# Two bookkeeping steps of an attention loop, placed later among its units

## The chip, the cores and the metric

The kernel runs on one core of a Trainium2 chip. The metric is the time of one execution on the device, in microseconds (us). A second number, the span, is what the profiler records from the first to the last instruction of one profiled execution; it is a little shorter than that execution's time.

## What is computed

Two blocks follow each other. The first is block-sparse attention over 4 batches, 8 heads, 768 tokens and 64 channels, with a mask made of 32 by 32 blocks. The second takes its output as 3072 rows of 512 numbers, gives each row to one of 8 experts by cosine similarity, and applies that expert's two-layer network.

```python
def _attn_ref(q, k, v, sampled_blocks):
    scores = np.matmul(q, k.transpose(0, 1, 3, 2)) / np.sqrt(D)
    ...
    scores = np.where(mask, scores, -1000000000.0)
    ...
    attn = np.exp(scores)
    attn = attn / (np.sum(attn, axis=-1, keepdims=True) + 1e-09)
    return np.matmul(attn, v)

def _moe_ref(x, expert_emb, tau, w1, w2):
    xn = x / (np.linalg.norm(x, axis=-1, keepdims=True) + 1e-06)
    en = expert_emb / (np.linalg.norm(expert_emb, axis=-1, keepdims=True) + 1e-06)
    logits = xn @ en.T / tau
    expert_idx = np.argmax(logits, axis=1)
    ...
    for e in range(E):
        mask = expert_idx == e
        h = np.maximum(x[mask] @ w1[e], 0.0)
        out[mask] = gate_w[mask, None] * (h @ w2[e])
```

## The kernel before

The attention handles heads in pairs: 16 pairs, four to a batch. Each pair has two halves of 384 queries, and each half runs over six chunks of 128 keys. One chunk of one half is a unit, so a half is 6 units, a pair 12, a batch 48, and there are 192 units. The loop in `attention_fast` (line 605) goes over them and issues, for each unit, the work of that unit and pieces of work that belong to other units.

The steps, with the names that the profile uses:

- `score_fast` (line 280) computes a unit's scores on TensorE into the tile `sc` (line 290), first the mask as a product of small bf16 matrices, then the queries and keys. ACT then takes the exponential into `e` (line 293). It is issued two units ahead. The pool of `sc` has two buffers, that of `e` four.
- `attend_fast` (line 297) adds `e` into a running sum `esum` on DVE (line 306 for the second unit of a half, line 308 for the later four) and multiplies `e` by the values into the accumulator `av` on TensorE (line 311). There is one accumulator buffer. At the sixth unit ACT copies one part of it (`part`, line 315) and DVE adds the two parts into `at` (line 317). The first `av` of the next half overwrites the accumulator, so it comes after that.
- `turn_fast` (line 260) turns half of the next pair's keys and queries by small matmuls into the tile `turn` (line 273). DVE copies the keys out (`kt`, line 276), ACT the queries (`qt`, line 277). It stands at the end of a half's sixth unit.
- `settle` (line 321) finishes a half. TensorE turns `at` back into rows of tokens and sums `esum` into denominators, both in the tile `back` (lines 339 and 346). DVE makes the denominators and their reciprocals (`dens` and `inv`, lines 349 to 352), the scaled rows `x` (line 354) and the products with the expert vectors (`part`, line 361, a second tile of that name). POOL squares `x` (`sq`, line 359), and DVE sums the squares (`nsq`, line 360).
- `route` (line 400) follows when a batch is complete. It is a chain of small operations on DVE with a power on POOL (`nrm`, line 410), which picks an expert for each token (`oh`, line 431). On ACT it takes one exponential of its logits `l` (line 434). The routed rows then go to memory by a DMA on the SP queue (line 438).
- `rank` (line 444) counts how many earlier tokens chose the same expert: six additions on POOL (`seen`, line 451), two products on TensorE into the tile `rk` (lines 453 and 454), and two DVE operations that read it (`mine` and `rank`, lines 455 and 456).

The tiles `turn`, `back` and `rk` all come from one pool, `small`, which has a single buffer of two banks; each of them waits until the one before has been read:

```python
def two_banks(k, name):
    return k.small.tile([P, 2, 512], F32, name=name, tag="small")
```

The order of the instructions on each engine's queue is made by a planner, which goes by the order of the program and by when it reckons an instruction to be ready. A queue then runs in that order. DVE's queue, for instance, has the sum of a half's second unit ahead of the copy `kt`, though the program issues `kt` first.

After the loop the last half is settled and the last batch routed and ranked (lines 620 to 622). `dispatch` then sorts the tokens into tiles of 128 by expert, and `experts` runs 27 of them (tiles `hp`, `h`, `yp`, `y`), with weights streamed from memory.

Of the kernel before, what the change touches and what calls it, by code (L numbers as in the profile page):

```python
# [23 lines left out]
NC = S // P  # L24
NPAIR = H // 2
# [31 lines left out]
def build_consts(k):  # L57
    nc, pool = k.nc, k.const
    k.ident = pool.tile([P, P], F32, name="ident")
    make_identity(nc, k.ident[:])  # L60
    k.ones = pool.tile([P, P], F32, name="ones")
    nc.vector.memset(k.ones, 1.0)
    k.half = pool.tile([P, NC], F32, name="half")
    nc.vector.memset(k.half, 0.5)

    k.before = pool.tile([P, P], F32, name="before")
    nc.gpsimd.memset(k.before, 1.0)
    nc.gpsimd.affine_select(out=k.before, in_=k.before, pattern=[[1, P]], compare_op=ALU.is_ge,
                            fill=0.0, base=-1, channel_multiplier=-1)
    k.rev = iota(k, "rev", [P, E], [[-1, E]], base=E)  # L70
    k.lane = iota(k, "lane", [P, P], [[1, P]])
    k.by_g = iota(k, "by_g", [P, N // G], [[G, N // G]])
    k.by_p = iota(k, "by_p", [P, NS + 1], [[P, NS + 1]])
    k.tile_no = iota(k, "tile_no", [P, NG], [[1, NG]])
    k.tok = iota(k, "tok", [P, NT], [[S, B], [1, NC]], base=-N, mult=NC)

    k.oh = pool.tile([P, NT, E], F32, name="oh")
    k.rank = pool.tile([P, NT], F32, name="rank")
    k.seen = pool.tile([P, NT + 1, E], F32, name="seen")
    nc.vector.memset(k.seen[:, 0, :], 0.0)  # L80


def load_ids(k):
    nc, pool = k.nc, k.setup
    k.ids = pool.tile([NB, NRAND], I32, name="ids")
    words = dataclasses.replace(k.blocks.tensor, shape=[NB, 2 * NRAND], dtype=I32)
    with nc.allow_non_contiguous_dma(reason="low words of the block numbers"):
        nc.sync.dma_start(out=k.ids, in_=bass.AP(tensor=words, offset=0, ap=[[2 * NRAND, NB], [2, NRAND]]))
# [57 lines left out]
def load_experts(k):  # L146
    nc, pool = k.nc, k.setup
    k.emb_rows = pool.tile([E, DM], F32, name="emb")
    nc.sync.dma_start(k.emb_rows, k.emb[:, :])
    k.tau_rows = pool.tile([E, 1], F32, name="tau")  # L150
    nc.sync.dma_start(k.tau_rows, bass.AP(tensor=k.tau.tensor, offset=0, ap=[[0, E], [1, 1]]))


def build_experts(k):
    nc, pool = k.nc, k.setup
    emb, tau = k.emb_rows, k.tau_rows
    sq = pool.tile([E, DM], F32, name="emb_sq")
    nrm = pool.tile([E, 1], F32, name="emb_nrm")
    nc.scalar.activation(sq, emb, ACT.Square, accum_out=nrm)
    nc.gpsimd.tensor_tensor(out=nrm, in0=nrm, in1=k.half[0:E, 0:1], op=ALU.pow)  # L160
    nc.vector.tensor_scalar(out=nrm, in0=nrm, scalar1=1e-6, scalar2=tau[:, 0:1], op0=ALU.add, op1=ALU.mult)
    nc.vector.reciprocal(out=nrm, in_=nrm)
    nc.vector.tensor_scalar(out=emb, in0=emb, scalar1=nrm[:, 0:1], scalar2=None, op0=ALU.mult)
    tp = two_banks(k, "tp")[:, 0]
    for c in range(ND):
        nc.tensor.transpose(tp[:, c * E:(c + 1) * E], emb[:, c * P:(c + 1) * P], k.ident[0:E, 0:E])
    k.en = k.const.tile([P, ND, E], F32, name="en")
    nc.vector.tensor_copy(out=k.en, in_=tp[:, 0:ND * E].rearrange("p (c e) -> p c e", e=E))
    k.back = k.const.tile([P, NPAIR, D + E], F32, name="back")
    for h in range(2):  # L170
        rows = slice(D * h, D * (h + 1))
        nc.vector.tensor_copy(out=k.back[rows, :, 0:D],
                              in_=k.ident[rows, rows].unsqueeze(1).broadcast_to([D, NPAIR, D]))
        nc.vector.tensor_copy(out=k.back[rows, :, D:D + E], in_=k.en[rows])


def load_pair(k, g, parts=(0, 1, 2), engine=None):
    b, j = g // NPAIR, g % NPAIR
    got = k.loaded.setdefault(g, [None, None, None])
    for i in parts:  # L180
        name, src = (("k", k.k), ("q", k.q), ("v", k.v))[i]
        t = k.ld.tile([P, 2, NC, D], F32, name=f"{name}ld", tag=f"{name}ld")
        (engine or k.nc.sync).dma_start(
            out=t.rearrange("p h c d -> p h (c d)"),
            in_=src[b, 2 * j:2 * j + 2].rearrange("h (p c) d -> p h (c d)", c=NC),
        )
        got[i] = t
# [72 lines left out]
def turn_fast(k, g, part):  # L260

    nc = k.nc
    if part == 0:
        k.turned[g] = [k.tp.tile([P, NC, 2, D], F32, name=f"{n}t", tag=f"{n}t") for n in ("k", "q")]
    ps = two_banks(k, "turn")[:, :, 0:2 * NQ * D].rearrange("p r (n c t) -> p r n c t", n=2, t=D)
    chunks = slice(part * NQ, (part + 1) * NQ)
    for n in range(2):
        src = k.loaded[g][n]
        for c in range(NQ):
            for r in range(2):  # L270
                toks = slice(D * r, D * (r + 1))
                for h in range(2):
                    nc.tensor.matmul(ps[D * h:D * (h + 1), r, n, c, :], lhsT=src[toks, h, part * NQ + c, :],
                                     rhs=k.ident[toks, toks], start=True, stop=True)
    kt, qt = [t[:, chunks].rearrange("p c r t -> p r c t") for t in k.turned[g]]
    nc.vector.tensor_copy(out=kt, in_=ps[:, :, 0])  # L276
    nc.scalar.mul(out=qt, in_=ps[:, :, 1], mul=SCALE)  # L277


def score_fast(k, u):  # L280

    nc = k.nc
    g, qh, kc = u // (2 * NC), u // NC % 2, u % NC
    kt, qt = [t.rearrange("p c r t -> p (c r t)") for t in k.turned[g]]
    ps = k.big.tile([P, 2, 512], F32, name="sc", tag="big")
    queries = slice(qh * HALF, (qh + 1) * HALF)
    quarters = [(h, r, slice(kc * P + D * r, kc * P + D * (r + 1))) for r in range(2) for h in range(2)]
    for rows, cols, first in ((k.kmask, k.qmask, True), (kt, qt, False)):
        for h, r, keys in quarters:
            nc.tensor.matmul(ps[D * r:D * (r + 1), h, 0:HALF], lhsT=rows[D * h:D * (h + 1), keys],  # L290
                             rhs=cols[D * h:D * (h + 1), queries], start=first, stop=not first)
    e = k.ep.tile([P, 2, HALF], F32, name="e", tag="e")
    nc.scalar.activation(e, ps[:, :, 0:HALF], ACT.Exp)  # L293
    k.es[u] = e
# [284 lines left out]
def attention_fast(n, ctx):  # L579
    def pool(name, bufs, **kw):  # L580
        return ctx.enter_context(n.tc.tile_pool(name=name, bufs=bufs, **kw))

    n.big, n.acc = pool("big_f", 2, space=PSUM), pool("acc", 1, space=PSUM)
    n.ld, n.tp, n.ep, n.sp = pool("ld", 3), pool("tp", 2), pool("ep", 4), pool("sp", 3)
    n.xp, n.rp = pool("xp", 2), pool("rp", 2)
    pairs = B * NPAIR
    units, per = pairs * 2 * NC, 2 * NC
    with n.tc.tile_pool(name="setup", bufs=1) as n.setup:
        load_ids(n)
        load_pair(n, 0, (0,))  # L590
        load_pair(n, 0, (1,), n.nc.scalar)
        load_pair(n, 0, (2,))
        load_experts(n)
        load_pair(n, 1)
        build_consts(n)
        build_mask(n)
        build_experts(n)
    zero = n.const.tile([1, XW], F32, name="zero")
    n.nc.vector.memset(zero, 0.0)
    n.nc.sync.dma_start(n.x_dram[N:N + 1, :], zero)  # L600
    for part in range(2):
        turn_fast(n, 0, part)
    score_fast(n, 0)
    score_fast(n, 1)
    for u in range(units):
        g = u // per
        if u % per == 0 and g + 2 < pairs:
            load_pair(n, g + 2)
        if u % NC == 1 and u > NC:
            settle(n, u // NC - 1)  # L610
        if u > NC and u % (per * NPAIR) == 2:
            route(n, u // (per * NPAIR) - 1)
        if u > NC and u % (per * NPAIR) == 4:
            rank(n, u // (per * NPAIR) - 1)
        attend_fast(n, u)
        if u + 2 < units:
            score_fast(n, u + 2)
        if u % NC == NC - 1 and g + 1 < pairs:
            turn_fast(n, g + 1, u % per // NC)
    settle(n, units // NC - 1)  # L620
    route(n, B - 1)
    rank(n, B - 1)
# [129 lines left out]
```

## Time and profile before

| | |
|---|---|
| median of 3 runs | 873.22 us (873.19 to 874.57) |
| the profiled execution | 872.45 us, span 870.6 us |
| mean granted TensorE clock | 0.957 of full speed |
| busy share of the span | PE 89%, PEld 58%, DVE 38%, ACT 23%, POOL 12% |
| the chain that ended last | PE 73%, DVE 9%, issue 6%, ACT 6% |
| its largest lines | `hp` 20%, `yp` 19%, `sc` 14%, `av` 12% |

PE is TensorE's matmuls, PEld its loads of the stationary operand, DVE VectorE, ACT ScalarE and POOL GpSimd. The attention lies between about 20 and 408 us; the expert tiles start at about 440 us. A timeline row gives the start, the busy time, the engine and line, the tile written and the tiles read, and in brackets how long the engine stood idle before it and what ended that. Rows of the same kind that follow each other closely are merged ("x24"). Two passes of a float32 matmul are two records, so the four `av` matmuls of a unit show as x8.

### The profile page before, as it was taken

What the parts mean: (1) busy time and instruction counts of PE and PEld (TensorE: products, weight loads), DVE (VectorE), ACT (ScalarE), POOL (GpSimd) and SP (SyncE); (2) the same over time, 40 slices, a digit from 0 to 9 for tenths busy, and PEclk for the clock granted to TensorE, in tenths of its full rate; (3) what the DMA queues carried; (4) which work ended last, traced back from release to release, by engine and by line L of the source; (5) the groups of instructions that cost most, each with busy time, mean ns of one, the idle gap of its engine ahead of it and who ended that gap; (6) DMA issues with size and microseconds to landing.
All of it is one profiled execution on the core that took longest, in us unless ns stands there. A gap on an engine that the chain in (4) does not pass through costs nothing.

```text
span 870.6 us, 22250 instructions
## 1 busy us (share of the span) xinstructions
PE 774.4 (89%) x10030; PEld 504.6 (58%) x10030; DVE 328.3 (38%) x641; ACT 200.0 (23%) x292; POOL 101.1 (12%) x139
## 2 busy tenths in 40 slices
PE   5999979998799979997459999999999999999883
PEld 2555535555455545553447676767676767676661
DVE  3666656666566665666711111111111111110100
ACT  3545434444344434443000000000000000000000
POOL 2000010001100010001010111101010101010100
PEclk9999989999899989999559999999999999999997
DMA  5111131111111130000179999989999999988780
GB/s 200 39 42 50 43 128 58 57 57 58 74 57 57 58 129 20 3 3 2 72 290 399 399 398 323 330 312 324 323 315 323 322 322 321 326 314 314 272 296 28
DMA packets 63810, 162.31 MB, mean 186 GB/s; under 512 B 2956, under 2 KB 15244, under 8 KB 63190
## 3 DMA queue, kind: packets, MB, share of 16 engines
q1 hardware_dynamic: 58950, 146.45, 47.9%
q0 software_dynamic: 4480, 13.91, 4.0%
q8 instruction: 82, 1.34, 0.6%
q10 hardware_dynamic: 272, 0.39, 0.1%
q14 instruction: 26, 0.21, 0.1%
HBM read 148.14 MB, written 13.38 MB: 186 GB/s over the span
## 4 chain that ended last, share of the span: by engine, by line
PE 73%; DVE 9%; issue 6%; ACT 6%; DMA 2%; POOL 2%; SPq 0%; POOLq 0%; DVEq 0%; ACTq 0%
PE hp L562 20%; PE yp L570 19%; PE sc L290 14%; PE av L311 12%; ACT e L293 3%; DVE esum L306 3%; PE back L346 2%; PE back L339 2%; DVE kt L276 2%; ACT qt L277 2%; PE slot_ps L514 1%; PE xg_ps L553 1%; DMA xg<-x_dram,slot 1%; DMA out_dram<-y,slot 1%; POOL seen L451 1%
## 5 line engine op out<-in xcount | busy, mean ns | idle before, releaser
L562 PEld LDWEIGHTS hp<-xgt,w 128*128 128x128 f32 x1728 | 199.9, 193 | 25.2 <-issue 11.0
L562 PE MATMUL hp<-xgt,w 128*128 128x128 f32 x1728 | 204.7, 277 | 8.8 <-ACT h L565 4.6
L570 PE MATMUL yp<-w,h 128*128 128x512 f32 x432 | 189.9, 592 | 0.0
L293 ACT ACTIVATE e<-sc 128x768 f32<-128x768 f32 x192 | 155.0, 810 | 150.3 <-PE sc L290 150.3
L311 PE MATMUL av<-e,vld 64*64 64x384 f32 x1536 | 162.9, 495 | 1.4 <-ACT e L293 1.0
L290 PE MATMUL sc<-qt,kt 64*64 64x384 f32 x1536 | 160.8, 490 | 0.0
L308 DVE TENSOR_TENSOR esum<-esum,e 128x768 f32<-128x768 f32 x128 | 122.3, 956 | 56.1 <-ACT e L293 53.1
L570 PEld LDWEIGHTS yp<-w,h 128*128 128x128 f32 x432 | 80.0, 190 | 90.4 <-issue 90.4
L565 ACT ACTIVATE h<-hp 128x512 f32<-128x512 f32 x27 | 16.1, 597 | 414.0 <-PE hp L562 399.7
L290 PEld LDWEIGHTS sc<-qt,kt 64*64 64x64 f32 x1536 | 59.3, 135 | 40.8 <-issue 38.7
L311 PEld LDWEIGHTS av<-e,vld 64*64 64x64 f32 x1536 | 53.0, 135 | 47.7 <-ACT e L293 20.7
L572 DVE TENSOR_SCALAR y<-yp,xg 128x512 f32<-128x512 f32 x27 | 20.3, 751 | 158.9 <-PE yp L570 158.9
L566 DVE TENSOR_SCALAR h<-hp 128x512 f32<-128x512 f32 x27 | 18.7, 692 | 161.2 <-PE hp L562 161.2
L573 POOL DMA_INDIRECT out_dram<-y,slot x27 | 27.4, 1016 | 353.5 <-DVE y L572 339.1
L359 POOL TENSOR_TENSOR sq<-x 128x384 f32<-128x384 f32 x32 | 26.4, 826 | 354.5 <-DVE part L361 209.7
L290 PE MATMUL sc<-qmask,kmask 64*64 64x384 bf16 x768 | 67.2, 329 | 0.0
L290 PEld LDWEIGHTS <-kmask 64*64 64x64 bf16 x768 | 24.8, 109 | 33.7 <-issue 33.7
L339 PEld LDWEIGHTS back<-back,at 64*64 64x64 f32 x768 | 14.7, 132 | 45.3 <-ACT qt L277 43.1
L339 PE MATMUL back<-back,at 64*64 64x72 f32 x768 | 19.3, 231 | 24.2 <-ACT qt L277 23.0
L306 DVE TENSOR_TENSOR esum<-e 128x768 f32<-128x768 f32 x32 | 30.7, 958 | 19.3 <-ACT e L293 19.3
L555 DVE COPY xgt<-xg_ps 128x512 f32<-128x512 f32 x27 | 18.5, 687 | 42.3 <-PE xg_ps L553 42.3
L538 POOL DMA_INDIRECT xg<-x_dram,slot x29 | 29.9, 1032 | 30.0 <-PE good_ps L378 21.4
(128 smaller groups left out, 375.4 us busy)
## 6 DMA issues: line engine op xcount, KB each, us to landing
w<-in_moe_w_dram SPq DMA_DIRECT2D x58, 2048.0 KB, 10.3
x_dram<-x SPq DMA_DIRECT2D x4, 1539.0 KB, 5.8
kld<-in_k_dram SPq DMA_DIRECT2D x16, 384.0 KB, 4.8
vld<-in_v_dram SPq DMA_DIRECT2D x16, 384.0 KB, 3.3
qld<-in_q_dram SPq DMA_DIRECT2D x15, 384.0 KB, 5.4
xg<-x_dram,slot POOLq DMA_INDIRECT x29, 7.3
out_dram<-y,slot POOLq DMA_INDIRECT x27, 7.5
qld<-in_q_dram ACTq DMA_DIRECT2D x1, 384.0 KB, 3.3
```

What stands on the lines that cost most here:

```text
L290: nc.tensor.matmul(ps[D * r:D * (r + 1), h, 0:HALF], lhsT=rows[D * h:D * (h + 1), keys], rhs=cols[D * h:D * (h + 1), queries], start=first ...
L293: nc.scalar.activation(e, ps[:, :, 0:HALF], ACT.Exp)
L306: nc.vector.tensor_tensor(out=k.esum, in0=k.first, in1=e, op=ALU.add)
L308: nc.vector.tensor_tensor(out=k.esum, in0=k.esum, in1=e, op=ALU.add)
L311: nc.tensor.matmul(k.av[D * h:D * (h + 1), r, 0:HALF], lhsT=v[D * r:D * (r + 1), h, kc, :], rhs=e[D * r:D * (r + 1), h, :], start=(kc == 0 ...
L339: nc.tensor.matmul(rows[D * s:D * (s + 1), t, h, :], lhsT=at[D * h:D * (h + 1), cols], rhs=k.back[D * h:D * (h + 1), j, :], start=True, st ...
L359: nc.gpsimd.tensor_tensor(out=sq, in0=x, in1=x, op=ALU.mult)
L538: nc.gpsimd.indirect_dma_start(out=x[:, :], out_offset=None, in_=k.x_dram[:, :], in_offset=bass.IndirectOffsetOnAxis(ap=k.slot[:, t:t + 1] ...
L562: nc.tensor.matmul(hp[:, f, :], lhsT=w1[:, d, f * P:(f + 1) * P], rhs=xt[:, d, :], start=(d == 0), stop=(d == ND - 1))
L570: nc.tensor.matmul(yp, lhsT=h[:, f, :], rhs=w2[:, f, :], start=(f == 0), stop=(f == NF - 1))
L572: nc.vector.tensor_scalar(out=y, in0=yp, scalar1=x[:, DM:XW], scalar2=None, op0=ALU.mult)
L573: nc.gpsimd.indirect_dma_start(out=k.out[:, :], out_offset=bass.IndirectOffsetOnAxis(ap=k.slot[:, i:i + 1], axis=0), in_=y[:, :], in_offse ...
```

## The change

Three conditions in the loop of `attention_fast` change. The settling of the half before, which stood ahead of a half's second unit, now stands ahead of its fourth. The routing of the batch before stood ahead of a batch's third unit and now stands ahead of its fifth, again one unit behind the batch's last settling. The rank products stood two units behind the routing and now stand ten units behind it, ahead of the batch's fifteenth unit. The lower bound on `u` is written anew; it lets the same three batches through. Nothing else differs, and no instruction is added or taken away.

```diff
-        if u % NC == 1 and u > NC:
+        if u % NC == 3 and u > NC:
             settle(n, u // NC - 1)
-        if u > NC and u % (per * NPAIR) == 2:
+        if u >= per * NPAIR and u % (per * NPAIR) == 4:
             route(n, u // (per * NPAIR) - 1)
-        if u > NC and u % (per * NPAIR) == 4:
+        if u >= per * NPAIR and u % (per * NPAIR) == 14:
             rank(n, u // (per * NPAIR) - 1)
```

## Rows read from the trace of the kernel before

**Rows 1.** Waits of TensorE, 31 to 398 us: total us, times, longest us

```profile
PE back L339 <- ACT qt L277: 23.0, 30, 0.8
...
```

**Rows 2.** Timeline of one ordinary half: start us, busy us, instructions, [idle before, releaser]

```profile
27.59 0.47 ACT L315 COPY part<-av 128x384 f32<-128x384 f32 x1
...
28.10 0.56 DVE L317 TENSOR_TENSOR at<-av,part 128x384 f32<-128x384 f32 x1 [0.81 <-ACT part L315]
...
28.79 0.83 PE L311 MATMUL av<-e,vld 64*64 64x384 f32 x8
...
29.18 0.96 DVE L306 TENSOR_TENSOR esum<-e 128x768 f32<-128x768 f32 x1 [0.52 <-ACT e L293]
...
30.06 0.55 DVE L276 COPY kt<-turn 128x384 f32<-128x384 f32 x1
30.64 0.49 ACT L277 ACTIVATE qt<-turn 128x384 f32<-128x384 f32 x1 [1.49 <-DVE kt L276]
31.03 0.81 ACT L293 ACTIVATE e<-sc 128x768 f32<-128x768 f32 x1
...
31.18 0.61 PE L339 MATMUL back<-back,at 64*64 64x72 f32 x24 [0.76 <-ACT qt L277]
...
31.87 0.96 DVE L308 TENSOR_TENSOR esum<-esum,e 128x768 f32<-128x768 f32 x1 [1.26 <-ACT e L293]
...
32.28 0.85 PE L311 MATMUL av<-e,vld 64*64 64x384 f32 x8
...
32.74 0.16 DVE L349 TENSOR_REDUCE dens<-back 128x6 f32<-128x12 f32 x1
...
35.34 2.01 DVE L308 TENSOR_TENSOR esum<-esum,e 128x768 f32<-128x768 f32 x2
...
38.12 0.82 PE L311 MATMUL av<-e,vld 64*64 64x384 f32 x8
...
40.27 0.83 PE L311 MATMUL av<-e,vld 64*64 64x384 f32 x8
...
```

**Rows 3.** Timeline of the last half of the attention

```profile
398.12 0.88 PE L311 MATMUL av<-e,vld 64*64 64x384 f32 x8 [0.44 <-DVE at L317]
...
400.67 0.85 PE L311 MATMUL av<-e,vld 64*64 64x384 f32 x8
...
404.25 3.07 DVE L308 TENSOR_TENSOR esum<-esum,e 128x768 f32<-128x768 f32 x3
...
```

**Rows 4.** Windows, halves with routing: us, busy PE PEld DVE ACT POOL, PEclk, DMA

```profile
111.55:130.77 19.22, 13.71 (x244) 7.46 (x245) 10.75 (x29) 5.64 (x10) 4.12 (x8) 0.82 0.29 113
211.14:231.72 20.58, 14.88 (x245) 7.73 (x245) 10.76 (x29) 5.75 (x10) 4.09 (x8) 0.83 0.27 106
312.09:331.71 19.62, 14.15 (x245) 7.55 (x245) 10.75 (x29) 5.74 (x10) 4.09 (x8) 0.83 0.29 113
...
```

**Rows 5.** Timeline of the first batch boundary

```profile
113.11 0.16 DVE L349 TENSOR_REDUCE dens<-back 128x6 f32<-128x12 f32 x1
...
119.67 0.24 ACT L434 ACTIVATE l<-l 128x48 f32<-128x48 f32 x1 [4.42 <-DVE pick L428]
...
119.82 1.49 ACT L293 ACTIVATE e<-sc 128x768 f32<-128x768 f32 x2
...
120.41 0.66 PE L453 MATMUL rk<-oh,before 128*128 128x48 f32 x2 [3.19 <-DVE oh L431]
...
120.64 0.96 DVE L308 TENSOR_TENSOR esum<-esum,e 128x768 f32<-128x768 f32 x1
...
123.14 1.56 PE L311 MATMUL av<-e,vld 64*64 64x384 f32 x8
...
127.61 0.52 PE L273 MATMUL turn<-ident,kld 64*64 64x64 f32 x24
...
```

**Rows 6.** Chain of waits at the same boundary: start us, us, what

```profile
120.72 0.95 POOL seen L451
...
121.74 0.21 POOL seen L451
...
```

## The prediction

> **What bounds the kernel now.** I read the waits first, then one ordinary half of the attention, then its boundaries. From 31 to 398 us TensorE's longest wait in total is that of `back` (the settling) for ACT's `qt`: 23.0 us in 30 times [rows 1]. Only `rk` (the rank products) waits beside it, at the three batch boundaries. Otherwise TensorE works, so time goes where its waits go.
>
> One half [rows 2], counted from the first `av` after a turning (28.79): the next such `av` is at 40.27, so a half takes 11.48. Its pieces: a unit of `av` and scores takes (38.12 - 32.28) / 4 = 1.46; the turning 40.27 - 38.12 - 1.46 = 0.69; a settling that waits for nothing is seen in the last half [rows 3], whose units stand 400.67 - 398.12 = 2.55 apart with it between, so 2.55 - 1.46 = 1.09. Six units, a turning and a settling make 8.76 + 0.69 + 1.09 = 10.54. The missing 0.94 is the wait ahead of `back`: 0.76 of idle, plus the overlap that a stopped pipeline loses. The reader should see why: turning and settling share the one buffer of the pool `small`, and between them stands a single unit. `kt` is copied on DVE only behind a running sum (`esum` at 29.18, then `kt` at 30.06), `qt` on ACT only behind `kt` (30.64), and `back` starts at 31.18, 0.05 after `qt` ends.
>
> The boundaries [rows 4]: the three halves with routing take 19.22, 20.58 and 19.62, together 59.42 - 3 x 11.48 = 24.98 more than ordinary ones, at a mean granted clock of 0.82 to 0.83. In the first [rows 5], `rk` waits 3.19 for `oh`, and its second half for `seen`; the next `av` comes at 123.14. But ACT stands still as well: 4.42 until the routing's exponential `l`, with two exponentials of scores queued behind it, which start only at 119.82. The `av` that TensorE has next needs the first of these.
>
> **The change, part by part.** *Settling two units later, ordinary half.* No instruction is added: its matmuls, six DVE operations and the POOL square move together; no DMA and no ACT operation is among them. `back` now stands three units behind the turning, and `qt` has been read long before. The 0.94 goes; what is late next is the exponential behind `qt`. It starts at 31.03 and ends at 31.84, 3.05 after the half's first `av`; with the hand-over of 0.05 the third `av` can start at 3.10, where its place would be 2 x 1.46 = 2.92. New wait 0.18 (bounds 0, if `kt` comes ahead of the sum, and 0.3). New half 10.54 + 0.18 = 10.72, that is 0.76 less.
>
> Does DVE keep up, now that the settling's chain stands nearer the end of the half? What counts is `at`, since `av` has a single accumulator: the next half's first `av` waits until `at` has read it. `at` starts 0.69 ahead of that `av` now (28.10 to 28.79) and may be 0.08 later at no cost (28.66 + 0.05 against 28.79). New: `back` at 3.10 + 1.46 = 4.56; `dens` came 1.56 behind `back`, behind a sum, so now at 6.1, or 6.6 if that sum waits for its own exponential (estimate). From `dens` to the next sum is 35.34 - 32.74 = 2.60, from a sum to the next operation 0.88: `at` could start at 9.6 to 10.1. TensorE's side wants it at 10.72 - 0.69 = 10.03. That is a tie within the 0.08, so I take no cost, with 0.05 per half as its upper bound. The turning needs the buffer only at 10.72 - 0.69 = 10.0; the chain has let it go before that next sum, by 9.2 at the latest.
>
> 30 halves have a turning ahead of a settling [rows 1]: 30 x 0.76 = 22.8 us. The last half had no such wait and gains nothing; its settling's 2.6 us on DVE now lie nearer the closing `at`, where three sums queue already [rows 3]: 0 to 0.5 lost, I take 0.2.
>
> *Rank products ten units behind the routing.* Their waits at the boundary go, but not the boundary's stall, because `l` stays where it is on ACT. Counted from the first `av` of that half, and with `dens` at 6.5 (from 6.1 to 6.6): `l` started 119.67 - 113.11 = 6.56 behind `dens`, the exponential behind it 6.71 behind. So unit 54's exponential starts at 13.2 and ends at 14.0. Behind it on ACT comes `part`, and `at` begins 0.51 after `part` does [rows 2], so at 14.5, ending at 15.1; `av` of unit 54 wants both and starts near 15.1 instead of 10.72. Stall 4.4 (bounds 3.3, if `part` came first and cost nothing, and 4.5). What moves to unit 62: two products, 0.66 for the first at the low clock [rows 5]; at the full clock, and partly within the 0.18 above, I take 0.8 for both (bounds 0.5 and 1.3). They take the `small` buffer between a turning two units before and a settling one unit behind; DVE's two small reads have that unit, 1.46, so I cost them at nothing; without it the settling would wait for them. POOL's six additions need only `oh`, nine units earlier. The DMA of the routed rows moves with the routing, two units, on an SP queue that next has a load eight units on; it costs nothing.
>
> The clock. At the first boundary, after the stall, two units took 127.61 - 123.14 = 4.47 instead of 2.92, so 1.55 was lost at the lower level (1.2 GHz; `av` took 1.56 instead of 0.83). The other boundaries were 1.36 and 0.40 longer with the same waits, so I estimate 2.9 and 1.95 for them. TensorE will again stand idle some 4.5 us, so I keep the mean, 2.1 (bounds 1.5 and 2.9).
>
> Excess of a boundary: 4.4 + 2.1 + 0.8 = 7.3, three of them 21.9, against 24.98: gain 3.1 only.
>
> *Sum.* -22.8 - 3.1 + 0.2 = -25.7 on the profiled execution's 872.45: 846.8. The median, 873.22, stands 0.77 above that execution, so I forecast 847.5. Its own range, from the bounds: 840 to 853.
>
> **A rule against the change.** At the first boundary the second addition of `seen` took 0.95 beside a running sum that ended at 120.64 + 0.96 = 121.60, the third took 0.21 [rows 5, 6]. So a POOL addition and a DVE sum did not run side by side there. Today the settling's square meets no sum: DVE waits for the square, and runs two sums in a row only behind it (35.34) [rows 2]. The Trainium skill, "SBUF — State Buffer", section "SBUF: two separate sides", says that the port they share is an exclusive lock, held for a whole instruction. The stretched addition agrees with it (0.95 against 0.21). By the order of now the rule costs nothing and the sum stays 847.5; with a sum ahead of the square it gives the 855 to 861 of rival 2.
>
> **The rivals.**
> 1. *The routing's `l` no longer blocks ACT.* The instruction order is a planner's, by readiness (`kt` stands behind a later unit's sum), so moving the ranks may put the exponentials of units 54 and 55 ahead of `l`. Then stall and clock loss go: 3 x 6.5 = 19.5 more, 828. Against: the distance from settling to routing, and the scores issued between them, stay the same. Chance 0.12.
> 2. *DVE's order around the settling differs by one sum.* If the sum of a half's fifth unit falls beside the square, one of the two waits, 0.95 - 0.21 = 0.74, and `nsq`, the next sum and `at` move back by as much from the early end of the reckoning (9.6): `at` at 10.34, half 10.34 + 0.61 = 10.95. That is some 0.25 x 30 = 7.5 more: 855; if the sum starts first and the square waits 0.96, `at` at 10.56 and half 11.17, 861. For: the chain has less room behind it now. Against: the sum ready ahead of `dens` stood ahead of it before (31.87). Chance 0.12.
> 3. *Slower: three sums queue behind the settling.* In the last half three sums ran in a row after `nsq` [rows 3], 1.055 apart. If the planner puts those of a half's last three units there, with `dens` behind no sum at about 5.9, the first starts at 5.9 + 2.60 = 8.5, `at` at 8.5 + 2 x 1.055 + 0.88 = 11.5, the next `av` at 12.1: halves 0.6 longer than now, 18 - 3 = 15, so 888 on the median. It decides from the point where `at` starts later than 11.0 after the half's first `av`. Against: before, the sums whose exponential was ready stood ahead of `dens`. Chance 0.04.
> 4. *The ranks do not really leave*, because TensorE's order still has them by the boundary: the boundaries keep their 24.98, time 850.6. Chance 0.06.
>
> **How the numbers follow.** Forecast 0.62, rivals 0.12, 0.12, 0.04 and 0.06, the rest 0.04 unnamed. The range takes in the forecast, rivals 2 and 4 and a part of rival 1: 835 to 861; what it leaves out is most of rival 1, rival 3 and the rest. A measurement here tells 0.2% (1.7 us) from no change. Slower: rival 3 and a quarter of the rest, 0.05; within 0.2%: 0.01; faster: 0.94.
>
> **What would show it.** Right: `back` waits for nothing; `av` waits some 0.2 for an exponential once a half; halves of 10.7; at the boundaries `av` waits more than 4 us for `at` or `e` with `l` ahead on ACT, at a granted clock below 1; `rk` waits nowhere but at the end. Wrong: `av` waiting for `at` in ordinary halves (rivals 2, 3), no idle ACT ahead of `l` (rival 1), `rk` still right behind `oh` (rival 4).

## The result, and the profile after

The changed kernel takes 845.3 us (four runs, 842.7 to 846.3), the one before 873.2 beside it (four runs, 873.0 to 874.6): a ratio of 0.967, with a 95% interval of 0.965 to 0.970. Forecast was 847.5 with a range of 835 to 861. The profiled execution took 844.77 us with a span of 843.0, so 27.6 less than the span before, 870.6.

The waits of TensorE over the attention, 31 to 385 us (columns: engine, tile and line, whom it waited for, total us, times, longest), answer to [rows 1]:

```profile
PE av L311 <- DVE at L317: 13.2, 4, 4.2
PE back L339 <- DVE at L317: 1.5, 1, 1.5
PE av L311 <- ACT e L293: 0.3, 1, 0.3
```

The 23.0 us of `back` behind `qt` are gone, and so is the wait of `rk` at the boundaries. Of the 13.2 that `av` waits for `at`, three times 4.2 lie at the batch boundaries; the rest is in the last half, where `back` waits its 1.5.

One ordinary half, as a timeline (start us, busy us, instruction, idle before it and its releaser), answers to [rows 2]:

```profile
71.67 0.88 PE L311 MATMUL av<-e,vld 64*64 64x384 f32 x8
...
73.49 0.49 ACT L277 ACTIVATE qt<-turn 128x384 f32<-128x384 f32 x1 [1.49 <-DVE kt L276]
...
73.88 0.80 ACT L293 ACTIVATE e<-sc 128x768 f32<-128x768 f32 x1
...
74.74 0.21 PEld L311 LDWEIGHTS av<-e,vld 64*64 64x64 f32 x8 [0.60 <-ACT e L293]
74.74 0.88 PE L311 MATMUL av<-e,vld 64*64 64x384 f32 x8
...
76.24 0.55 PE L339 MATMUL back<-back,at 64*64 64x72 f32 x24
...
77.39 0.96 DVE L308 TENSOR_TENSOR esum<-esum,e 128x768 f32<-128x768 f32 x1 [0.65 <-ACT e L293]
...
78.27 0.16 DVE L349 TENSOR_REDUCE dens<-back 128x6 f32<-128x12 f32 x1
...
79.60 0.83 POOL L359 TENSOR_TENSOR sq<-x 128x384 f32<-128x384 f32 x1 [9.90 <-DVE part L361]
...
80.46 0.55 DVE L360 TENSOR_REDUCE nsq<-sq 128x3 f32<-128x384 f32 x1 [0.89 <-POOL sq L359]
...
81.80 0.55 DVE L317 TENSOR_TENSOR at<-av,part 128x384 f32<-128x384 f32 x1
...
82.40 0.88 PE L311 MATMUL av<-e,vld 64*64 64x384 f32 x8
```

`back` starts 2.75 behind `qt` and waits for nothing. The half takes 82.40 - 71.67 = 10.73, against 11.48 before. The third `av` stands 74.74 - 71.67 = 3.07 behind the first instead of 2.92; only the row of its weight load names the exponential behind `qt` as the cause. No sum runs beside the square on POOL. `at` ends at 82.35, 0.05 ahead of the next `av`: DVE and TensorE are done together. That 0.05 is also what lies between `at` and an `av` that waits for it (118.93 to 118.98 at the boundary below), so `at` has no room left, though no idle time is shown; before the change there was 0.13 (28.66 to 28.79).

Windows of the first and the third boundary half (the second takes 16.63), of the half with the ranks behind the first, and of an ordinary half (us; busy us and count of PE, PEld, DVE, ACT, POOL; granted clock; share of the DMA engines; GB/s) answer to [rows 4]:

```profile
108.44:125.08 16.64, 12.41 (x244) 6.93 (x240) 10.30 (x28) 5.76 (x9) 4.09 (x8) 0.90 0.24 99
...
292.98:309.59 16.61, 12.40 (x244) 6.92 (x240) 10.30 (x28) 5.76 (x9) 4.07 (x8) 0.90 0.24 98
125.08:136.32 11.24, 11.24 (x248) 6.64 (x244) 8.04 (x16) 5.62 (x8) 0.83 (x1) 1.00 0.35 108
76.24:86.97 10.73, 10.73 (x244) 6.19 (x240) 7.30 (x14) 5.62 (x8) 0.83 (x1) 1.00 0.35 111
```

A boundary half is 5.90 longer than an ordinary one, and the ranks add 11.24 - 10.73 = 0.51 later: 6.4 each, where it was 8.3. The first boundary, as a timeline, answers to [rows 5]:

```profile
113.52 1.35 POOL L410 TENSOR_TENSOR nrm<-nrm,half 128x6 f32<-128x6 f32 x1 [0.89 <-DVE nrm L409]
...
116.81 0.18 DVE L428 TENSOR_SCALAR pick<-l 128x48 f32<-128x48 f32 x1
117.02 0.24 ACT L434 ACTIVATE l<-l 128x48 f32<-128x48 f32 x1 [4.94 <-DVE pick L428]
...
117.17 0.79 ACT L293 ACTIVATE e<-sc 128x768 f32<-128x768 f32 x1
...
117.51 0.21 DVE L431 TENSOR_TENSOR oh<-pick,mx 128x48 f32<-128x48 f32 x1
...
117.86 0.47 ACT L315 COPY part<-av 128x384 f32<-128x384 f32 x1
...
118.37 0.56 DVE L317 TENSOR_TENSOR at<-av,part 128x384 f32<-128x384 f32 x1 [0.34 <-ACT part L315]
...
118.98 1.11 PE L311 MATMUL av<-e,vld 64*64 64x384 f32 x8 [4.23 <-DVE at L317]
```

ACT stands still for 4.94 us until the routing's `l`; an exponential, then `part`, then `at`, then `av` follow it. But DVE's own queue has the routing chain (`nsq` to `oh`) ahead of `at` as well. Which of the two queues sets the end can't be seen from this one timeline; two of the experiments ask that.

The account of the span: 30 halves at 0.75 make 22.5, the boundaries 24.98 - 3 x 6.41 = 5.75, and the last half loses 0.33 (10.18 from its first `av` to the closing `back`, now 10.51). Together 27.9, and the spans differ by 27.6.

### The profile page after: what moved, and what is told of

Same layout as the page of the kernel before. It is cut to its first block, busy times and chain, and to the rows that moved or that the text cites. A ratio compares the mean times of both kernels' runs of the same rounds, so it can differ in the third digit from the quotient of the medians.

```text
span 843.0 us, 22253 instructions
## 1 busy us (share of the span) xinstructions
PE 771.0 (91%) x10030; PEld 506.1 (60%) x10030; DVE 325.6 (39%) x641; ACT 200.2 (24%) x292; POOL 101.2 (12%) x139
## 4 chain that ended last, share of the span: by engine, by line
PE 82%; issue 6%; DVE 5%; DMA 2%; ACT 2%; POOL 1%; SPq 0%; POOLq 0%; ACTq 0%; DVEq 0%
PE hp L562 21%; PE yp L570 20%; PE sc L290 17%; PE av L311 15%; PE turn L273 3%; PE back L346 2%; PE slot_ps L514 1%; PE back L339 1%; DVE esum L308 1%; PE xg_ps L553 1%; ACT e L293 1%; DMA out_dram<-y,slot 1%; DMA xg<-x_dram,slot 1%; POOL nrm L410 1%; DMA emb<-in_moe_expert_emb_dram 1%
## 5 line engine op out<-in xcount | busy, mean ns | idle before, releaser
L311 PE MATMUL av<-e,vld 64*64 64x384 f32 x1536 | 164.7, 499 | 14.2 <-DVE at L317 13.2
L311 PEld LDWEIGHTS av<-e,vld 64*64 64x64 f32 x1536 | 50.5, 134 | 67.4 <-ACT e L293 24.5
L360 DVE TENSOR_REDUCE nsq<-sq 128x3 f32<-128x384 f32 x32 | 17.7, 554 | 24.2 <-POOL sq L359 24.2
L277 ACT ACTIVATE qt<-turn 128x384 f32<-128x384 f32 x32 | 15.7, 491 | 47.4 <-DVE kt L276 47.4
```

The source lines that it names most:

```text
L311: nc.tensor.matmul(k.av[D * h:D * (h + 1), r, 0:HALF], lhsT=v[D * r:D * (r + 1), h, kc, :], rhs=e[D * r:D * (r + 1), h, :], start=(kc == 0 ...
```

## The experiments

Each kernel ran four times, beside seven runs of the kernel before (median 872.1 for the first four kernels, 873.1 for the last four). All diffs are against the changed kernel.

**Each half of the change alone.** First, settling and routing as changed, with the ranks two units behind the routing as before:

```diff
-        if u >= per * NPAIR and u % (per * NPAIR) == 14:
+        if u >= per * NPAIR and u % (per * NPAIR) == 6:
```

> Settling and routing as in the changed kernel, the rank products again two units behind the routing. Theory (the settling brings nearly all of it): halves of 10.73 us as in the changed kernel, so 30 x 0.75 = 22.5 less than before; the three boundaries stay near what they cost before (8.3 us each over an ordinary half), because `l` on ACT and `at` hold TensorE whether or not the ranks stand there. About 850 us. Rival (the ranks at the boundary were the larger part, 25 us in all): the halves give little and the time is near 865 to 870.

Measured: 855.6 us (854.8 to 857.0), ratio 0.981 (0.979 to 0.983), where about 850 was expected. The ordinary halves are 10.73, as expected; the boundaries cost more than expected. TensorE's waits over the attention, and windows from the first boundary's `av` on:

```profile
...
PE rk L453 <- ACT qt L277: 1.7, 3, 0.6
...
```

```profile
118.86:121.90 3.04, 2.48 (x10) 1.22 (x10) 1.43 (x2) 0.56 (x2) 1.05 (x2) 0.50 0.97 409
121.90:126.40 4.50, 4.50 (x33) 2.71 (x36) 0.74 (x3) 0.81 (x1) 0.00 (x0) 0.50 0.12 47
...
```

The wait of `av` for `at` is 13.2 as in the changed kernel. New is that `rk` comes right behind a turning, waits 0.56 for `qt`, and that the granted clock stays at the lower level (0.50) for 7.5 us. In the changed kernel the first 4.65 us behind the same stall have a mean of 0.63 (again a window):

```profile
118.98:123.63 4.65, 4.65 (x41) 2.17 (x44) 2.38 (x3) 1.37 (x3) 1.04 (x2) 0.63 0.75 311
```

A mean of 0.63 is 0.74 of that time at the lower level, 3.4 us. The 4.1 us more of it in the first kernel, at half speed, make 2 us; with the 0.56 that is most of the 3.3 by which the boundary half and the one behind it are longer here (31.22 against 16.64 + 11.24 = 27.88). With its ranks beside the boundaries this kernel thus pays 3.3 us more at each, 10 in all. That the ranks bring on the longer time at the lower clock is not shown: over the 4.23 us of the stall, before any rank product, the mean granted clock is 0.75 here and 1.00 in the changed kernel, at all three boundaries.

Second, the ranks alone: settling and routing where they stood before, ranks thirteen units behind the routing.

```diff
-        if u % NC == 3 and u > NC:
+        if u % NC == 1 and u > NC:
-        if u >= per * NPAIR and u % (per * NPAIR) == 4:
+        if u >= per * NPAIR and u % (per * NPAIR) == 2:
-        if u >= per * NPAIR and u % (per * NPAIR) == 14:
+        if u >= per * NPAIR and u % (per * NPAIR) == 15:
```

> Settling and routing as before, the rank products moved alone, thirteen units behind the routing. Theory: the 0.76 ahead of each `back` stays, halves 11.48; a boundary still stalls about 3.7 us, because `av` waits for an exponential that stands behind `l` on ACT, and loses some 1.5 at the low clock; with 0.5 for the ranks in their new place a boundary costs 5.7 instead of 8.3. About 865 us (864 to 867). Rival (the waits of `rk`, with what they do to the clock, are the whole boundary): 25 us less, about 848.

Measured: 866.5 us (865.0 to 868.2), ratio 0.994 (0.992 to 0.996). Waits of TensorE, 31 to 398 us, beside the two lines on `rk` from the kernel before, then windows of the first and the third boundary half (the second is like the first, 16.88):

```profile
PE back L339 <- ACT qt L277: 23.0, 30, 0.8
PE av L311 <- ACT e L293: 10.3, 3, 3.4
...
```

```profile
PE rk L453 <- DVE oh L431: 9.5, 3, 3.2
PE rk L454 <- POOL seen L451: 4.7, 3, 1.7
```

```profile
112.69:129.56 16.87, 12.59 (x241) 6.47 (x241) 10.43 (x27) 5.70 (x10) 4.91 (x8) 0.90 0.33 129
...
308.65:323.84 15.19, 10.98 (x240) 6.04 (x241) 10.43 (x27) 5.64 (x10) 4.89 (x8) 1.00 0.37 145
```

The wait of `back` stays to the tenth, so it belongs to the settling's place alone. With `rk` out of the way, `av` waits 3.4 for `e` instead, 10.3 in all where `rk` waited 14.2: most of the stall is the boundary's, not the ranks'. The third half, with a like wait but an undisturbed clock, is 1.7 shorter, which prices the clock loss of one stall.

The two moves by themselves give 1.9% and 0.6%, which add up to 2.5%; both at once give 3.3%. They are not independent. An ordinary half takes 10.73 in the first kernel as in the changed one, so the difference lies at the boundaries, where `rk`, right behind a turning, brings a wait of its own and the clock stays low for longer.

**The settling's place.** One unit earlier, then one unit later than in the change (routing one unit behind it in both; the ranks at 16 in the first):

```diff
-        if u % NC == 3 and u > NC:
+        if u % NC == 2 and u > NC:
...
+        if u >= per * NPAIR and u % (per * NPAIR) == 3:
...
+        if u >= per * NPAIR and u % (per * NPAIR) == 16:
```

> Settling ahead of a half's third unit, one unit earlier than in the changed kernel; routing one behind it, ranks at the same distance from a turning or a settling. Theory: the settling's 1.09 us of TensorE work now lie ahead of the third `av`, whose exponential comes late behind `qt`; so that wait of 0.18 goes, `qt` is read before `back` is due (2.3 against 2.9 us after the half's first `av`), and `at` is off DVE's edge: halves of 10.54 to 10.58, 30 x 0.17 = 5 less than the changed kernel, about 840 us. Rival 1 (DVE's chain or another wait sets the half): 845, no change. Rival 2 (the wait on `qt` returns): halves of 11 and more, over 850.

Measured: 839.5 us (838.9 to 841.1), ratio 0.963 (0.961 to 0.965). An ordinary half takes 10.49, less than the 10.54 that the prediction summed without any wait:

```profile
84.27:94.76 10.49, 10.49 (x245) 6.20 (x241) 7.39 (x13) 5.62 (x9) 0.83 (x1) 1.00 0.14 48
```

With the settling ahead of the third `av`, the exponential behind `qt` is covered by it, and `at` ends 0.13 ahead of the next `av` (91.72 to 91.85) as it did before the change. So the 0.24 by which a half of the changed kernel is longer was the price of going one unit too far. The wait behind `qt` is 0.15 of it; how the rest divides, between `at` at its limit and matmuls that overlap less, is not separated by these runs.

```diff
-        if u % NC == 3 and u > NC:
+        if u % NC == 4 and u > NC:
...
+        if u >= per * NPAIR and u % (per * NPAIR) == 5:
```

> Settling ahead of a half's fifth unit, one unit later than in the changed kernel, routing one behind it. Theory (the half already stands at DVE's edge): `dens` at 8.0 us after the half's first `av`, the squares' sum 2.1 later, `at` only behind it at 10.6, the next half's first `av` at 11.2 instead of 10.73: 30 x 0.48 = 14 more, about 859 us, with `av` waiting for `at` in ordinary halves. Rival (DVE has slack left, the settling may stand anywhere behind the turning): 845, no change.

Measured: 858.3 us (857.4 to 860.3), ratio 0.984 (0.982 to 0.987). TensorE's waits over the attention, and the end of one half on the timeline:

```profile
PE av L311 <- DVE at L317: 24.3, 30, 4.3
```

```profile
84.19 0.55 DVE L360 TENSOR_REDUCE nsq<-sq 128x3 f32<-128x384 f32 x1 [0.89 <-POOL sq L359]
...
84.66 0.55 DVE L317 TENSOR_TENSOR at<-av,part 128x384 f32<-128x384 f32 x1
...
85.26 0.88 PE L311 MATMUL av<-e,vld 64*64 64x384 f32 x8 [0.43 <-DVE at L317]
```

A half takes 11.15. Now `av` waits for `at` in every ordinary half, 0.43 each time: `nsq`, held up by the square, stands ahead of `at`. This is the far side of the tie that the prediction saw. A half is bound by the turning's chain on one side and by `at` on the other, and the unit chosen by the change is the last at which `av` does not stand idle for `at`.

**What holds the boundary.** The prediction has `l` on ACT hold the exponentials, `part` and `at`. If that is all (theory B), taking `l` off ACT's queue at the boundary removes the stall; if DVE's order holds `at` too (theory A), it removes little. In this kernel the gate rows (the exponential of `l`, its sum, the reciprocal and the row DMA) are a function of their own, called behind `rank`, and a bias of 0 times the rank keeps the planner from moving them forward:

```diff
+def gate_rows(k, b):
+    nc, p, x, l = k.nc, k.rp, k.x[b], k.l.pop(b)
     gate = p.tile([P, NC], F32, name="gate")
-    nc.scalar.activation(l, l, ACT.Exp)
+    zero = p.tile([P, 1], F32, name="late")
+    nc.vector.tensor_scalar(out=zero, in0=k.rank[:, b * NC:b * NC + 1], scalar1=0.0, scalar2=None, op0=ALU.mult)
+    nc.scalar.activation(l, l, ACT.Exp, bias=zero[:, 0:1], scale=1.0)
...
             rank(n, u // (per * NPAIR) - 1)
+            gate_rows(n, u // (per * NPAIR) - 1)
```

> The changed kernel, with the routing's exponential `l` and the gate made from it moved behind the rank products (a zero made from the ranks is its bias, so it can't come sooner). ACT then has nothing between the exponentials at a boundary. Theory A (DVE's queue holds the boundary as well: `at` stands behind the whole routing chain, its `oh` last): `av` still waits for `at`, about 3.7 us instead of 4.2, and the clock still falls; 843 us (841 to 845). Theory B (`l` on ACT alone holds it, as the prediction had it): stall and clock loss go, 3 x 5.9 = 17.7 less, about 827 us.

Measured: 842.2 us (841.0 to 842.8), ratio 0.965 (0.964 to 0.967), where theory A said 843. The first boundary:

```profile
113.29 0.47 ACT L315 COPY part<-av 128x384 f32<-128x384 f32 x1
...
117.42 0.21 DVE L431 TENSOR_TENSOR oh<-pick,mx 128x48 f32<-128x48 f32 x1
...
117.55 0.55 DVE L317 TENSOR_TENSOR at<-av,part 128x384 f32<-128x384 f32 x1
...
118.15 0.88 PE L311 MATMUL av<-e,vld 64*64 64x384 f32 x8 [3.49 <-DVE at L317]
```

`part` is now done at 113.76, 4.6 us earlier. `at` has its inputs then, but stands in DVE's queue behind the routing chain until 117.55. ACT is free and TensorE still waits 3.49 instead of 4.23. Each queue runs in its written order; the Trainium skill, "Perfetto Trace Analysis", section "Tensor Engine Instruction (MATMUL, LD_WEIGHTS)", calls those of ACT and DVE strict first-in-first-out, and this row agrees: 3.8 us from the end of `part` to the start of `at`.

The gain itself is small. The interval overlaps that of the changed kernel (0.965 to 0.970); the three waits give back 2.2 us (13.2 to 11.0 over the attention), and in the profiled execution the second boundary half ran at a clock of 1.00 (14.18 us), the others at 0.89 (15.90 and 15.87).

The counterpart leaves `l` in the chain and pushes the chain behind `at`: the power's result is added to 0 times `at`, the routing stands two units later, the ranks at 20. It does not clear DVE's queue alone, since `l` is made by the chain and so moves behind `at` with it.

```diff
     nc.gpsimd.tensor_tensor(out=nrm, in0=nrm, in1=k.half, op=ALU.pow)
+    if after is not None:
+        nc.vector.scalar_tensor_tensor(out=nrm, in0=after[:, 0:NC], scalar=0.0, in1=nrm, op0=ALU.mult, op1=ALU.add)
...
-            route(n, u // (per * NPAIR) - 1)
+            route(n, u // (per * NPAIR) - 1, n.done[u // NC - 1][0])
```

> The changed kernel, with the routing's DVE chain behind its power made to wait for the `at` of the half under way (a zero made from `at` is added to the norms), `l` in its place in the chain; ranks six units later than in the changed kernel. DVE's queue then has `at` ahead of the chain. Theory A (the order on DVE holds the boundary): `av` no longer waits for `at`; late next is the exponential behind `qt`, since `kt` stands behind the chain's first half: about 1.3 us, too short for the clock to fall. A boundary costs 1.8 instead of 6.4: 831 us (829 to 835). Theory B (`l` on ACT alone): `l` still stands on ACT ahead of `qt` and the exponentials behind it, and comes no sooner, so the boundary keeps 4 us and its low clock: 842 to 845.

Measured: 838.0 us, from 834.2 to 846.4, ratio 0.961 (0.953 to 0.968): between the two theories, and wide. Behind the first boundary:

```profile
118.95 0.55 DVE L276 COPY kt<-turn 128x384 f32<-128x384 f32 x1
...
119.54 0.49 ACT L277 ACTIVATE qt<-turn 128x384 f32<-128x384 f32 x1 [1.34 <-DVE kt L276]
...
119.92 1.51 ACT L293 ACTIVATE e<-sc 128x768 f32<-128x768 f32 x2
...
120.78 0.88 PE L311 MATMUL av<-e,vld 64*64 64x384 f32 x8 [1.98 <-ACT e L293]
```

Two units get through, then the next thing in line is late: `kt` is now the copy that queues behind the chain on DVE, `qt` and the exponential queue behind it on ACT, and the third `av` waits 1.98. So `av` no longer waits for `at`, as theory A had it, but what comes next costs more than the 1.3 it gave, and the clock, which it took to stay up, falls at two of the three boundaries. Windows of the first and the third boundary half, each with the half behind it, tell of the spread:

```profile
109.27:122.75 13.48, 11.42 (x244) 6.31 (x240) 10.91 (x29) 5.75 (x9) 5.32 (x7) 0.96 0.16 63
122.75:136.33 13.58, 13.57 (x244) 7.77 (x240) 7.11 (x14) 5.61 (x8) 1.12 (x3) 0.78 0.46 146
...
293.15:306.13 12.98, 10.95 (x244) 6.20 (x240) 10.44 (x29) 5.75 (x9) 4.83 (x7) 1.00 0.13 51
306.13:316.86 10.73, 10.73 (x244) 6.12 (x240) 7.31 (x14) 5.61 (x8) 1.58 (x3) 1.00 0.36 132
```

After nearly the same wait the clock fell behind the first boundary (0.78, 2.9 us lost while TensorE had no wait at all) and behind the second (0.77), and not behind the third. The four executions differ in their mean clock in the same way: 0.954 with 846.4, 0.959 with 841.3, 0.967 and 0.968 with 834.6 and 834.2.

The order on DVE's queue shows something else. The routing's first operations still run ahead of `at` (`nrm`, line 409, at 114.08; `at` at 115.06), though they are now called behind it. Only what the data ties to `at` came later.

**Both queues cleared.** The gate behind the ranks as above, and the chain held behind `kt` instead of `at` (routing two units later and ranks at 20, as in the counterpart):

```diff
+        if u >= per * NPAIR and u % (per * NPAIR) == 6:
+            route(n, u // (per * NPAIR) - 1, n.turned[g + 1][0].rearrange("p c r t -> p (c r t)")[:, 0:NC])
```

> Both: the gate behind the ranks, and the routing's DVE chain behind the copy `kt` of the half's turning. Then at a boundary neither `at`, `kt` and `qt` nor the exponentials have a routing step ahead of them; the chain delays running sums only. Theory A: a boundary costs the rank products' 0.5 and little else, TensorE's clock stays at full: 3 x 5.7 = 17 less than the changed kernel, about 828 us (826 to 831). Rival (the routing's work has to be paid somewhere, since DVE is the edge of a half): `at` of the next half is late by the chain's 2.5 us, 835 to 837.

Measured: 829.2 us (828.3 to 830.1), ratio 0.950 (0.948 to 0.952). Windows of the boundary half, the next, and the one with the ranks:

```profile
109.36:120.16 10.80, 10.72 (x245) 6.26 (x241) 9.36 (x25) 5.62 (x8) 3.21 (x3) 1.00 0.03 7
120.16:131.44 11.28, 10.71 (x244) 6.29 (x240) 7.91 (x15) 5.73 (x8) 3.67 (x7) 1.00 0.36 108
131.44:142.68 11.24, 11.24 (x248) 6.64 (x244) 8.01 (x17) 5.95 (x9) 0.83 (x1) 1.00 0.01 1
```

This boundary costs 33.32 - 3 x 10.73 = 1.13 in all, and the clock stays full. 0.51 of it are the ranks; 0.55 lie in the second window, where `av` waits 0.57 for an `at` that the chain has made late. So the rival was right about the kind of cost, but it is 0.57 and not 2.5. By the ratios, freeing ACT alone gave 0.2% of the time before, the counterpart 0.7%, both moves together 1.7%. Whether the gate has to move at all once the chain stands behind `kt` is not shown: no run holds the chain there with `l` left in it.

The same with the settling at the third unit (`u % NC == 2`) and the ranks at 22:

> The kernel with gate and chain moved as in the run before, and the settling ahead of a half's third unit besides. The two gains touch different waits, so they should add: 845 - 17 - 5.7 = about 822.5 us (820 to 826). If the settling's DVE chain and the routing's chain then meet in the same stretch: 826 to 829, no better than the run before.

Measured: 825.0 us (824.1 to 825.8), ratio 0.946 (0.944 to 0.947). It is the fastest of all, some 20 us under the changed kernel, though the settling's place added 4.2 us and not the 5.7 expected. What is left for TensorE to wait over the attention (31 to 300 us) is small ("issue" is a wait for nothing that the profile shows):

```profile
PE turn L273 <- issue: 2.1, 2, 1.2
PE av L311 <- DVE at L317: 1.5, 3, 0.5
```

## Why the prediction was right

- *The wait ahead of `back`* goes in all 30 halves, as forecast, and comes back nowhere. The half is 10.73 against 10.72. The new wait behind `qt` measures 0.15 (0.18 was forecast), and it is gone in the kernel with the settling one unit earlier. That the halves agree to 0.01 is in part luck: that kernel's half, in which TensorE waits for nothing, takes 10.49, so the base of 10.54 was 0.05 too high, and what the change adds to it is 0.24 and not 0.18.
- *DVE keeps up, at a tie.* Forecast was `dens` at 6.1 to 6.6 behind the first `av` and `at` at 9.6 to 10.1; measured 6.60 and 10.13. Both lie at the late end, which was to come if the sum ahead of `dens` waits for its own exponential, as it does (77.39). `at` came at the very limit of what costs nothing. The one-unit-later kernel shows how narrow the tie is: 0.43 a half.
- *The boundary.* The stall of 4.4 came out as 118.98 - 103.86 - 10.73 = 4.39, and the `av` at 15.12 behind the half's first (15.1). The path over ACT that the sum followed is the one that ended last. But the reason given was half of it. The step "the boundary's stall stays because `l` stays where it is on ACT" describes the later of two holds. DVE's order, with `at` behind the whole routing chain, holds `at` almost as long, and without `l` most of the stall remains. The number took no harm only because the hold that was overlooked ends 0.8 us sooner (without `l`, `at` starts at 117.55 instead of 118.37). Rival 1 did not occur, and at 19.5 us for `l` leaving ACT's queue it was priced wrong as well: moving `l` away gave 2 to 3 us, and with the chain moved behind `kt` besides about 15.
- *Mis-sized terms.* The clock's loss was put at 2.1 per boundary, the mean of before; it measured 16.64 - 10.73 - 4.39 = 1.52, near the lower bound of 1.5. The ranks were put at 0.8 and cost 0.51, at the lower bound of 0.5, without a wait. The closing half lost 0.33 instead of 0.2. The first two make a boundary 6.4 instead of 7.3, 2.7 us in all; less 0.3 from the halves and 0.1 from the closing half, that leaves about the 2.2 us by which the forecast was too high. The four runs spread over 3.7 us, so an agreement to 0.1 means little here.
- *Two sums.* Rival 2 took the half's 10.95 - 10.72 as 0.25; it is 0.23, which gives 854 instead of 855. And the bounds of the single terms, added up, give about 836 to 857, wider than the forecast's own 840 to 853.
- *The rule against the change.* No POOL square met a sum: all 32 took 0.83. The Trainium skill's exclusive port ("SBUF — State Buffer", section "SBUF: two separate sides") was therefore not tested by this change. The kernel with both queues cleared has a row that agrees with it: its power on POOL (114.44) started 0.16 behind a running sum (114.28, 0.95 long) and took 1.99, where it took 1.35 beside no sum.
- Rivals 2, 3 and 4 did not occur: `av` stands idle for `at` in no ordinary half, and the ranks stand ten units behind the routing.

## What to carry to other kernels

When two steps share a single buffer, place them by both distances: from the last reader of the one, and to the next deadline of the other; here a half took 10.49 at the best place, 11.48 one unit earlier, 10.73 one later and 11.15 two later. When a stall stands behind an idle engine, look at the order of every queue that the late instruction passes before calling the idle one its cause: if two queues hold it, clearing one may show almost nothing, here 0.2% against 1.7% for both. And where a planner orders the queues by readiness, moving a call in the program may leave its instructions where they were, as with `nrm` above; a data dependency does move them.

## What was not expected of the hardware

Two stalls of the same length do not cost the same. With a wait of 3.4 each, two boundaries of the ranks-alone kernel ran at a mean clock of 0.90 and one at 1.00, 1.7 us apart. The same stall of 4.23 left the clock at 1.00 while it lasted in the changed kernel and at 0.75 in the one with the ranks beside the boundary. And behind a wait of only 1.98 the clock of another kernel fell to 0.78 over a whole half without a wait. What decides between them these runs leave open. So a stall can cost more afterwards, in the clock, than while it lasts: 2.9 behind 2.0.
